# Attention and gated FFN in one kernel: two x tiles turned by DMA instead of on TensorE, six FFN units in halves, one load and four stores moved

## The chip, the cores and the metric

The kernel runs on one core of one Trainium2 chip. The metric is the device time of one execution in microseconds (us); lower is better. One execution in each case was also recorded by the profiler. The record marks each run as fast or slow by its time and its granted clock. Engines: PE is TensorE, PEld its weight loads, DVE is VectorE, ACT is ScalarE, POOL is GpSimd, SP is SyncE, whose work in these traces is to issue DMAs.

## The reference

```python
# q, k, v: (8 batches, 8 heads, 576, 64) float32
phi(x) = concat(relu(x) * cos, relu(x) * sin)        # by position in the sequence
kv  = phi(k)^T v ;  z = sum over s of phi(k)
x   = (phi(q) kv) / (phi(q) z + 1e-6)                # -> (4608 tokens, 512)
out = (gelu(x w_gate) * (x w_val)) w_out             # w_gate, w_val: 512 x 1536; w_out: 1536 x 512
```

A batch has 576 tokens. The FFN works on nine blocks of 512 tokens, so a block straddles two batches. Block 1 is the last 64 tokens of batch 0 and the first 448 of batch 1.

## The kernel before

Per batch: `prep` makes phi(q) and phi(k) (cosine half on VectorE, sine half on ScalarE); q is transposed to `qT`; `kv_unit` makes kv; `nm_unit(b, t)` makes one tile x(b, t) of 128 tokens; the tile must be transposed ("turned") to become columns of `xT`, the moving operand of the FFN. Per block: 12 units `gv_unit` (gate and value matmuls, gelu on ScalarE, product on VectorE), then four output tiles `o_part`.

There are two ways to turn a tile. One holds TensorE (0.22 us a tile in the trace before) and needs a copy out of PSUM by ScalarE (L361, 0.37 to 0.63 us each there); the other is a DMA in SP's queue:

```python
def turn_x(b, t):
    x = xs.pop((b, t))
    for blk, c, o, m in pieces(b, t):                  # a tile that straddles blocks: two pieces
        nc.sync.dma_start_transpose(out=xT_block(blk)[:, :, c:c + m], in_=x[o:o + m, :])

def turn_x_pe(b, t, to, copy):
    x = xs.pop((b, t))
    p = bank16(to)[:, 0:CT * 128].rearrange("p (c n) -> p c n", c=CT)
    for ct in range(CT):                               # four transposes
        nc.tensor.transpose(out=p[:, ct, :], in_=x[:, ct * 128:(ct + 1) * 128], identity=ident)
    for blk, c, o, m in pieces(b, t):
        copy(xT_block(blk)[:, :, c:c + m], p[:, :, o:o + m])
```

A unit can run in halves, `gv_unit(n, unit, half * HALF, HALF)`: first the left 256 columns of several units, then the right 256. In block 1 the left half needs tiles 0 and 1 of batch 1, the right half tiles 1, 2 and 3 (of tile 3 the first 64 tokens; the rest belongs to block 2).

The stretch between the blocks, and the start of block 1 (before):

```python
    # GpSimd's queue: weights, q(1), k(1), v(1), then the loads of batch 2
    for name in ("q", "k"):
        for m in (0, 2):
            load(nc.gpsimd, name, 2, m, m + 2)
    for m in (0, 2):
        load(nc.gpsimd, "v", 2, m, m + 2)
    # ... block 0 ...
    order = (
        [("q", 0, 2, 0, 6), ("q", 2, 4, 0, 7), ("o", 0, 0), ("k",), ("o", 1, 0)]
        + [("q", 0, 2, 4, 2), ("o", 2, 0), ("q", 2, 4, 4, 3), ("o", 3, 0), ("o", 0, 4)]
        + [("q8", 2), ("o", 1, 4), ("o", 2, 4), ("kv",), ("q2", 0, 2), ("o", 3, 4)]
        + [("nm", 0, 2), ("o", 0, 8), ("nm", 1, 6), ("o", 1, 8), ("xt", 0, 4), ("nm", 2, 2)]
        + [("q2", 2, 3), ("o", 2, 8), ("xt", 1, 5), ("nm", 3, 6), ("q2", 3, 4), ("o", 3, 8)]
        + [("xt", 2, 4)]
    )
    # "q": transposes of phi(q(1)); "o": a third of an output tile; "q2": preparation of q(2);
    # "nm": nm_unit(1, t); "xt": turn_x_pe(1, t, bank)
    for m in (0, 2):
        load(nc.sync, "q", 3, m, m + 2)
    # ... block 1, unit jt:
            heads = (0, 2, 4, 2)[n] if n < 4 else 0          # units in halves
                    if n == 1:
                        j = JA + 2 * jt + i                  # preparation of q(2), one position
                        prep("q", b, 1, (j,), eng=nc.scalar)
                        prep("q", b, 0, (j,))
                        if jt == i == 0:
                            turn_x_pe(1, 3, 5, act_copy)     # tile 3 after the first half unit
                if n == 1 and jt == 2:
                    # (last position of q(2)) ...
                    turn_q(b)                                # q(2)'s turn, two DMA transposes by SP
                    nm_unit(1, NT - 1)
```

Each `o_part` that ends a tile also issues the stores of the tile before (`flush`), in SP's queue.

## Time and profile before

| | before |
|---|---|
| median of 3 runs, known at the prediction | 326.14 us (325.64 to 326.65) |
| median of 6 runs, with the result | 326.61 us (325.64 to 327.38) |
| span of the profiled run | 323.9 us |
| TensorE busy | 316.8 us, 98% |
| chain of waits on TensorE | 93% |

The first lines are from the page of the kernel before: busy time with share of the span and number of instructions; then the chain of work that ended last, by engine (a q behind an engine's name is its instruction queue, "issue" is time in which nothing that the profile shows was waited for); then the group of the gate matmuls (count, busy us, mean ns, idle time before them).

```profile
PE 316.8 (98%) x2451; PEld 164.5 (51%) x2451; DVE 170.3 (53%) x407; ACT 159.3 (49%) x336; POOL 26.0 (8%) x43
PE 93%; DMA 2%; DVE 2%; SPq 1%; issue 0%; DVEq 0%
L400 PE MATMUL ps<-xT,wg_sb 128*128 128x512 bf16 (+1 forms) x456 | 110.2, 364 | 0.0
```

With 98% of the span busy and 93% of the chain, TensorE bounds the kernel. Only what comes off TensorE's own sequence, or makes it stand still, moves the time.

The timeline of TensorE before, where block 1 starts (start, duration with the modelled tail, instruction):

```profile
53.44 1.02 PE L430 MATMUL ps<-wo_sb,hT 128*128 128x512 bf16 x4
54.30 0.39 PE L357 MATMUL ps<-ident,x_sb 128*128 128x128 bf16 x4
54.53 0.60 PE L400 MATMUL ps<-xT,wg_sb 128*128 128x256 bf16 x4
54.96 0.60 PE L400 MATMUL ps<-xT,wv_sb 128*128 128x256 bf16 x4
55.40 0.39 PE L357 MATMUL ps<-ident,x_sb 128*128 128x128 bf16 x4
55.62 0.60 PE L400 MATMUL ps<-xT,wg_sb 128*128 128x256 bf16 x4
56.06 0.60 PE L400 MATMUL ps<-xT,wv_sb 128*128 128x256 bf16 x4
56.62 0.60 PE L400 MATMUL ps<-xT,wg_sb 128*128 128x256 bf16 x4
```

Read such a list by its start times: the groups overlap (those of half matmuls last 0.60 us in the list and start 0.44 us apart), so a group costs the distance to the next start. Turning tile 2 costs the distance from 54.30 to 54.53, 0.22 us before rounding, and tile 3 the same. A group of four half matmuls costs 0.44 us, so a half unit 0.87. The third half unit starts 0.12 us late.

### The profile page before, as it was taken

To read this page: it belongs to the slowest core of one execution; us is meant where nothing else is said; L and a number is where in the kernel's file an instruction comes from. 1 tells how busy PE (TensorE), PEld (TensorE's weight loads), DVE (VectorE), ACT (ScalarE), POOL (GpSimd) and SP (SyncE) were. 2 spreads that over 40 slices of the span, in tenths; PEclk is the share of its full clock that TensorE was granted. 3 is DMA by queue.
4 is the path that set the end of the run, shared out by engine and by line. 5 is a ranking of instruction groups with operands and counts; after the bars stand their busy time and mean duration, and the time that the engine had idled before them with its cause. 6 is when DMAs were issued, how large, how long until landed. Compare 5 with 4: busy or idle time off the path is not lost.

```text
span 323.9 us, 6340 instructions
## 1 busy us (share of the span) xinstructions
PE 316.8 (98%) x2451; PEld 164.5 (51%) x2451; DVE 170.3 (53%) x407; ACT 159.3 (49%) x336; POOL 26.0 (8%) x43
## 2 busy tenths in 40 slices
PE   8899999999999999999999999999999999999995
PEld 3574556555754564545544554445544444444443
DVE  5854677759665952793586348544532222222211
ACT  7864858946466832673457336633222332222220
POOL 6684410000000000000000000000000000000000
PEclk9999999999999999999999999999999999999999
DMA  7999999842999689938957990543431111111124
GB/s 274 249 186 273 297 352 366 230 111 51 323 216 354 166 147 383 201 83 251 330 96 157 383 232 1 137 102 78 85 73 33 34 32 32 35 32 32 34 65 98
DMA packets 69102, 53.57 MB, mean 165 GB/s; under 512 B 45392, under 2 KB 54352, under 8 KB 69072
## 3 DMA queue, kind: packets, MB, share of 16 engines
q1 hardware_dynamic: 59264, 41.23, 48.1%
q0 software_dynamic: 9648, 11.80, 15.7%
q8 instruction: 19, 0.31, 0.4%
q10 hardware_dynamic: 160, 0.13, 0.1%
q14 instruction: 11, 0.09, 0.1%
HBM read 37.75 MB, written 9.44 MB: 146 GB/s over the span
## 4 chain that ended last, share of the span: by engine, by line
PE 93%; DMA 2%; DVE 2%; SPq 1%; issue 0%; DVEq 0%
PE ps L400 57%; PE ps L430 28%; PE ps L282 3%; PE ps L241 3%; DMA vf<-in_v_dram 2%; PE ps L204 1%; PE ps L372 1%; PE ps L697 1%; SPq L80 1%; PE ps L357 0%; DVE qp L162 0%; DVE x_sb L322 0%; DVE vx L179 0%; DVE x_sb L295 0%; DVE qT L486 0%
## 5 line engine op out<-in xcount | busy, mean ns | idle before, releaser
L409 DVE TENSOR_TENSOR hT<-gel,ps 128x512 bf16<-128x512 f32 (+1 forms) x114 | 74.1, 650 | 128.9 <-PE ps L400 126.0
L408 ACT ACTIVATE gel<-ps 128x512 f32<-128x512 f32 (+1 forms) x114 | 64.8, 569 | 109.7 <-PE ps L400 108.0
L400 PE MATMUL ps<-xT,wv_sb 128*128 128x512 bf16 (+1 forms) x456 | 110.2, 364 | 0.0
L400 PE MATMUL ps<-xT,wg_sb 128*128 128x512 bf16 (+1 forms) x456 | 110.2, 364 | 0.0
L430 PE MATMUL ps<-wo_sb,hT 128*128 128x512 bf16 x420 | 105.8, 379 | 0.0
L400 PEld LDWEIGHTS <-wv_sb 128*128 128x128 bf16 x456 | 44.6, 98 | 47.0
L400 PEld LDWEIGHTS <-wg_sb 128*128 128x128 bf16 x456 | 44.0, 98 | 46.1
L430 PEld LDWEIGHTS <-hT 128*128 128x128 bf16 x420 | 38.3, 98 | 39.4
L439 ACT COPY o_sb<-ps 128x512 f32<-128x512 f32 x34 | 19.9, 587 | 29.9 <-PE ps L430 27.6
L160 ACT ACTIVATE qp<-qf,sin_t 128x256 bf16<-128x256 f32 x72 | 32.0, 501 | 0.4 <-DMA qf<-in_q_dram 0.4
L160 ACT ACTIVATE kp<-kf,sin_t 128x256 bf16<-128x256 f32 (+1 forms) x73 | 29.9, 479 | 0.9 <-DMA kf<-in_k_dram 0.9
L295 DVE TENSOR_TENSOR x_sb<-ps,rec 128x512 bf16<-128x512 f32 x38 | 26.3, 691 | 1.3
L162 DVE TENSOR_SCALAR qp<-qf,cos_t 128x256 bf16<-128x256 f32 x71 | 21.8, 353 | 2.3 <-DMA qf<-in_q_dram 2.3
L282 PEld LDWEIGHTS <-qT 128*128 128x128 bf16 x304 | 14.6, 98 | 7.9 <-ACT qT L486 0.3
L162 DVE TENSOR_SCALAR kp<-kf,cos_t 128x256 bf16<-128x256 f32 x63 | 18.3, 349 | 0.0
L282 PE MATMUL ps<-kv_sb,qT 128*128 128x65 bf16 x304 | 16.0, 194 | 0.0
L179 DVE CAST vx<-vf 128x1152 bf16<-128x1152 f32 (+1 forms) x15 | 12.0, 804 | 0.8 <-DMA vf<-in_v_dram 0.8
L250 ACT CAST kv_sb<-ps 128x260 bf16<-128x260 f32 x14 | 4.6, 383 | 12.9 <-PE ps L241 12.9
L241 PEld LDWEIGHTS <-kp 64*128 64x128 bf16 x504 | 8.5, 95 | 3.0 <-issue 3.0
L140 PE MATMUL ps<-dummy 128*128 128x512 bf16 x27 | 8.4, 457 | 1.5 <-POOL dummy L113 1.5
L241 PE MATMUL ps<-vx,kp 64*128 64x65 bf16 x504 | 9.3, 191 | 0.0
L294 DVE RECIPROCAL rec<-den 128x8 f32<-128x8 f32 x38 | 7.7, 203 | 1.3
(60 smaller groups left out, 100.6 us busy)
## 6 DMA issues: line engine op xcount, KB each, us to landing
out_dram<-o_sb SPq DMA_DIRECT2D x70, 128.0 KB, 2.6
kf<-in_k_dram SPq DMA_DIRECT2D x12, 576.0 KB, 6.2
vf<-in_v_dram SPq DMA_DIRECT2D x12, 576.0 KB, 8.3
qf<-in_q_dram SPq DMA_DIRECT2D x10, 576.0 KB, 5.0
qf<-in_q_dram POOLq DMA_DIRECT2D x4, 576.0 KB, 12.2
kf<-in_k_dram POOLq DMA_DIRECT2D x4, 576.0 KB, 12.5
vf<-in_v_dram POOLq DMA_DIRECT2D x4, 576.0 KB, 12.8
wg_sb<-in_moe_w_gate_dram POOLq DMA_DIRECT2D x6, 256.0 KB, 6.4
```

The costliest lines, as they stand in the source:

```text
L140: nc.tensor.matmul(bank(to), lhsT=dummy[:, 0:128], rhs=dummy, start=True, stop=True)
L160: nc.scalar.activation(o, i, AF.Relu, scale=tab[:, j:j + 1])
L162: (eng or nc.vector).tensor_scalar(o, i, 0.0, tab[:, j:j + 1], op0=ALU.max, op1=ALU.mult)
L179: copy(vx_tiles[b % 2][:, m0:m1, j0:j1, 0:D], staged["v", b][:, m0:m1, j0 * D:j1 * D].rearrange("p m (j d) -> p m j d", d=D),)
L241: nc.tensor.matmul(bank(6 + i)[:, m * (D + 1):(m + 1) * (D + 1)], lhsT=kp[rr, m, j, :], rhs=vx[rr, m, j, :], start=(j == 0), stop=(j == R ...
L282: nc.tensor.matmul(bank(b0 + h // 4)[:, (h % 4) * (D + 1):(h % 4 + 1) * (D + 1)], lhsT=q_cols(b, t, h), rhs=kv_sb[b][:, h // 2, h % 2, :], ...
L295: nc.vector.tensor_tensor(x, nm[:, :, :, 0:D], rec[:, :, :, None].to_broadcast([128, 2, 4, D]), op=ALU.mult,)
L400: nc.tensor.matmul(bank(b0 + g)[:, 0:w], lhsT=wt[:, ct, js], rhs=xt[:, ct, c0:c0 + w], start=(ct == 0), stop=(ct == CT - 1),)
L408: nc.scalar.activation(gel[:, 0:w], bank(b0)[:, 0:w], AF.Gelu)
L409: nc.vector.tensor_mul(hT[n][:, jt, c0:c0 + w], gel[:, 0:w], bank(b0 + 1)[:, 0:w])
L430: nc.tensor.matmul(bank(to), lhsT=hT[n][:, jt, tt * 128:(tt + 1) * 128], rhs=wo_sb[:, jt, :], start=(jt == 0), stop=(jt == JT - 1),)
L439: copy(o_sb, bank(to))
```

## The change

The intent is to take two groups of transposes off TensorE (x tiles 2 and 3 of batch 1) and give them to the DMA. A DMA turn takes longer (2.3 to 2.5 us from issue to landing in the trace before, for those issued from 69 to 80 us), so the units that need these tiles must start later (six units in halves, left halves first), and SP's queue must be free when the turns are issued (behind bulk loads in it a turn took 10.0 us there, issued at 96.4 us): q(3)'s load goes to the GpSimd queue, of block 0's stores tile 0's go ahead of the turns, tile 1's behind them, and those of tiles 2 and 3 behind q(2)'s turn. The preparation of q(2) is rearranged so that q(2)'s turn is issued after unit 1 instead of unit 2, and k(2) is prepared position by position. The core of the diff (cut where marked):

```diff
+    def flush(n=4):                                   # stores in parts
+        for i, o_sb in stores[:n]:
             store((nc.sync, nc.sync), i, o_sb)
+        del stores[:n]
@@ o_part
-            flush()
+            if i == 1 or n > 0:
+                flush()
@@ GpSimd queue
+    for name, b in (("q", 2), ("k", 2), ("v", 2), ("q", 3)):
         for m in (0, 2):
+            load(nc.gpsimd, name, b, m, m + 2)
@@ order
-        + [("q8", 2), ("o", 1, 4), ("o", 2, 4), ("kv",), ("q2", 0, 2), ("o", 3, 4)]
-        + [("nm", 0, 2), ("o", 0, 8), ("nm", 1, 6), ("o", 1, 8), ("xt", 0, 4), ("nm", 2, 2)]
-        + [("q2", 2, 3), ("o", 2, 8), ("xt", 1, 5), ("nm", 3, 6), ("q2", 3, 4), ("o", 3, 8)]
-        + [("xt", 2, 4)]
+        + [("q8", 2), ("o", 1, 4), ("o", 2, 4), ("kv",), ("o", 3, 4)]
+        + [("nm", 0, 2), ("o", 0, 8), ("nm", 1, 6), ("q2", 0, 2), ("o", 1, 8), ("xt", 0, 4), ("nm", 2, 2), ("xd", 2)]
+        + [("o", 2, 8), ("xt", 1, 5), ("q2", 2, 3), ("nm", 3, 6), ("xd", 3), ("q2", 3, 4), ("o", 3, 8)]
+        if what == "xd":
+            turn_x(1, a[0])
+    flush(1)
-    for m in (0, 2):
-        load(nc.sync, "q", 3, m, m + 2)
@@ block 1
-            heads = (0, 2, 4, 2)[n] if n < 4 else 0
+            heads = (0, 6, 4, 2)[n] if n < 4 else 0
-                        if jt == i == 0:
-                            turn_x_pe(1, 3, 5, act_copy)
+                if n == 1 and jt == 1:
+                    turn_q(b)
                 if n == 1 and jt == 3:
                     turn_x(1, NT - 1)
+                    flush()
... (preparation of q(2) in units 0 and 1, of k(2) from unit 2 on)
```

More of the change, by code (lines that the diff above doesn't have):

```diff
@@ L420, in store @@
             eng.dma_start(out=dst, in_=o_sb[64 * n:64 * n + 64, c0:c1])
-    def flush():
-        for i, o_sb in stores:
+    def flush(n=4):
+        for i, o_sb in stores[:n]:
             store((nc.sync, nc.sync), i, o_sb)
-        stores.clear()
+        del stores[:n]
     def o_part(i, jts, to, copy):
@@ L474 @@
     load_wo(8, 4)
-    for name in ("q", "k"):
+    for name, b in (("q", 2), ("k", 2), ("v", 2), ("q", 3)):
         for m in (0, 2):
-            load(nc.gpsimd, name, 2, m, m + 2)
-    for m in (0, 2):
-        load(nc.gpsimd, "v", 2, m, m + 2)
+            load(nc.gpsimd, name, b, m, m + 2)
     def turn_j(b, m0, m1, js, to, copy):
@@ L581 @@
             turn_x_pe(1, a[0], a[1], act_copy)
-    for m in (0, 2):
-        load(nc.sync, "q", 3, m, m + 2)
+        if what == "xd":
+            turn_x(1, a[0])
+    flush(1)
     def prep_third(name, b, i):
@@ L623 @@
                     gv_unit(n, unit, half * HALF, HALF)
-                    if n == 1:
-                        j = JA + 2 * jt + i
-                        prep("q", b, 1, (j,), eng=nc.scalar)
-                        prep("q", b, 0, (j,))
-                        if jt == i == 0:
-                            turn_x_pe(1, 3, 5, act_copy)
-            if jt % 3 == 1:
+                    if n == 1 and jt < 2:
+                        js = ((4,), (5,), (6,), (7, 8))[2 * jt + i]
+                        prep("q", b, 1, js, eng=nc.scalar)
+                        prep("q", b, 0, js)
+                    if n == 1 and jt > 1:
+                        j = 2 * jt - 4 + i
+                        prep("k", b, 0, (j,))
+                        prep("k", b, 1, (j,), eng=nc.scalar)
+            if jt % 3 == 1 and n > 1:
                 flush()
             if b < B:
+                if n == 1 and jt == 1:
+                    turn_q(b)
                 if n == 1 and jt == 2:
-                    prep("q", b, 0, (R - 1,))
-                    prep("q", b, 1, (R - 1,), eng=nc.scalar)
-                    turn_q(b)
                     nm_unit(1, NT - 1)
@@ L653 @@
                     kv_unit(b)
-                i = jt - 1 - n if n <= 2 else -1
-                if 0 <= i < 3:
-                    prep_third("k", b, i)
+                if n == 1 and jt == 6:
+                    prep("k", b, 0, (R - 1,))
+                    prep("k", b, 1, (R - 1,), eng=nc.scalar)
+                if n == 2 and 3 <= jt < 6:
+                    prep_third("k", b, jt - 3)
                 i = 2 * (jt - 5) if n == 1 else jt - (4 if n == 2 else 0)
```

## The prediction

> **What bounds the kernel.** TensorE: busy 316.8 of 323.9 us (98%, busy times), 93% of the chain of waits; the granted clock is full in every slice. In the timeline of 39 to 62 us, the stretch that the change touches, each of its groups starts where the one before ends; I find two gaps of some 0.1 us (before batch 1's kv unit at 47.23 and the third half unit at 56.62). ScalarE is slack on average (49%) but full from 52 to 58 us (table by windows).
>
> **What the change does, costed from the timeline.**
> 1. Tiles 2 and 3 are no longer turned on TensorE: each group of four transposes holds it 0.22 us (54.30 to 54.53, 55.40 to 55.62). Removed: 0.45 us, on the critical path. ScalarE loses three copies out of PSUM, off the path.
> 2. Four more units run in halves. A half unit takes 0.87 us, a whole one 1.73: 0.02 us more each, 0.05 to 0.1 us in all, on the path. This buys time: the second column half, which alone needs tiles 2 and 3, starts six half units (5.2 us) into the block, about 59.5 us instead of 56.5.
> 3. Three DMA transposes are added in SP's queue (tile 3 in two pieces), 1.2 us of issue each. On an idle queue such a turn lands 2.3 to 2.5 us after issue (69 to 80 us); behind bulk loads in SP's own queue it took 10.0 (at 96.4). So moving q(3)'s load away, and holding back stores, matters. The GpSimd queue ran dry about 54.3 us; q(3)'s 1.18 MB at the 425 GB/s of 50 to 52 us add 2.8 us: it runs to about 57, beside the turns. [...] the turns should be slowed, not queued behind; this trace has only stores as a parallel: 4.5 us under load against 2.6.
> 4. q(2)'s turn is issued about 60 us instead of 61.5, and k(2)'s preparation is spread. Both have slack: q(2)^T is first read about 72 us, kv(2) runs at 69.
>
> **Deadline.** x of tile 2 should be ready about 53.4 us, of tile 3 about 54.7. With 4 to 5 us under load they land by 58 to 59.5, against a need at 59.5: little slack; one chance in three of a stall of 0.3 to 1 us. Second tight place: the first half unit needs ScalarE's copy of tile 1 just as TensorE arrives (54.1 against 54.3).
>
> **Sum.** -0.45 + 0.08, and +0.1 for expected stalls: -0.3 us. From 326.14 I predict 325.8 us, range 325.1 to 326.9. Faster by over 2%: 1%; within 2%: 98%; slower by over 2%: 1%. The affected stretch is 20 us of a full TensorE; 6.5 us cannot come of it.
>
> **What would show it.** 2,475 matmuls instead of 2,451 (8 transposes fewer, 32 half matmuls more); 37 turns of x by DMA instead of 34; 118 gelus instead of 114. The first half unit starts about 54.3 us instead of 54.53; block 2's first unit about 77.7 instead of 78.04, and everything later keeps that offset; span about 323.6. The three turns land 3 to 5 us after issue. If TensorE idles before the seventh half unit, released by the DMA of xT, the deadline failed; if it idles before the first or third on ScalarE, the sines did it.
>
> **What would make it wrong.** Turns much slower beside the GpSimd queue's loads (8 to 10 us) would stall TensorE 3 to 4 us: 329. q(3)'s load delaying v(2) or k(2) would show as VectorE waiting before their preparation. A start-up that differs by chance would hide all of it: the three runs of before spread by 1.0 us.

## More of the kernel before

The DMA queues before, in the window from 53 to 54 us (queue, packets, MB, share of the 16 engines' time). q0 is the GpSimd queue, q1 SP's:

```profile
q0 software_dynamic: 79, 0.30, 75.4%
q1 hardware_dynamic: 44, 0.08, 21.7%
```

From 50 to 53 us q1 had no packet at all, although SP had issued two stores at 51.3 and 51.9 us. They landed at 55.98 and 56.28.

## The result, and the profile after

| | before | after |
|---|---|---|
| median of 6 runs | 326.61 us (325.64 to 327.38) | 326.56 us (326.15 to 326.95) |
| ratio | | 1.0000, 95% interval 0.9982 to 1.0018 |
| span of the profiled run | 323.9 us | 324.0 us |

A ratio here and below is the mean time of one kernel's fast runs over the mean of the other's of the same rounds, so it is not quite the ratio of the medians. All outputs are right.

The time is the same within 0.18%, which is 0.6 us; the predicted 0.3 us is less than this measurement can tell. So the traces have to say what happened. The same lines of the page after, and from its list of groups the line of the gate matmuls (busy, mean ns, idle before and what ended it):

```profile
PE 314.1 (97%) x2438; PEld 167.4 (52%) x2475; DVE 171.2 (53%) x411; ACT 159.0 (49%) x337; POOL 29.5 (9%) x45
PE 90%; DMA 6%; issue 1%; ACT 1%; POOL 1%; DVE 0%; SPq 0%; DVEq 0%
L400 PE MATMUL ps<-xT,wg_sb 128*128 128x512 bf16 (+1 forms) x463 | 109.9, 357 | 1.6 <-DMA xT<-x_sb 0.9
```

The weight loads count 2,475 matmuls, as predicted (37 matmul records are missing from the trace). The chain of waits now has 6% on DMA (v(0)'s load, a weight load and the turn of x, 2% each), and in the list of groups an idle time of 0.9 us ended by the DMA of xT appears, where the same line before had 0.0. The timeline of TensorE after shows where:

```profile
53.28 0.81 PE L430 MATMUL ps<-wo_sb,hT 128*128 128x512 bf16 x3
53.93 0.60 PE L400 MATMUL ps<-xT,wg_sb 128*128 128x256 bf16 x4
54.37 0.60 PE L400 MATMUL ps<-xT,wv_sb 128*128 128x256 bf16 x4
...
58.73 0.60 PE L400 MATMUL ps<-xT,wv_sb 128*128 128x256 bf16 x4
59.17 0.42 PE L282 MATMUL ps<-kv_sb,qT 128*128 128x65 bf16 x8
60.46 0.60 PE L400 MATMUL ps<-xT,wg_sb 128*128 128x256 bf16 x4 [0.87 <-DMA xT<-x_sb]
```

The two groups of transposes (L357) are gone and the first six half units follow each other without a gap. Then the seventh, which is the first to need tiles 2 and 3, starts at 60.46 us. The x unit before it (L282) costs 0.26 us, so it could have started at 59.43: TensorE lost 1.03 us.

What SP issued after:

```profile
50.93 1.47 SPq L420 DMA_DIRECT2D out_dram<-o_sb  x2
53.37 3.88 SPq L349 DMA_TRANSPOSE xT<-x_sb  x3
57.34 1.18 SPq L420 DMA_DIRECT2D out_dram<-o_sb  x2
59.67 8.09 SPq L193 DMA_TRANSPOSE qT<-qp  x2
```

The three turns, issued at 53.37, 54.76 and 56.01, landed at 60.11, 60.33 and 60.54 us. From the view of the line that issues them, window 53 to 61:

```profile
DMA to landing us min/median/max: 4.5/5.6/6.7
```

Three DMAs issued 1.3 us apart that land 0.2 us apart did not take 6.7, 5.6 and 4.5 us each. This looks like a wait for one common event; the experiments test which.

To compare traces, take two numbers from TensorE's timeline. The start of the first of q(1)'s 16 transposes, which comes before anything that the change touches, is **S**; what lies before it is called the start-up here (two profiles of the changed kernel have S at 38.71 and 40.24). The time from there to block 2's first half unit is the **stretch**; it holds everything that the change does. What follows block 2's start took 245.7 to 246.0 us in all traces but one (246.3).

| | S | stretch | S + stretch |
|---|---|---|---|
| before | 39.08 | 38.96 | 78.04 |
| after | 38.71 | 39.49 | 78.20 |

So in its profiled run the changed kernel was 0.53 us slower in the stretch that it was meant to shorten, and an early start hid most of it. The sum is: -0.45 for the transposes, +0.08 for more halves, -0.12 for the gap before the third half unit that is gone, +1.03 for the wait: +0.54.

### The profile page after: what moved, and what is told of

Same layout as the page of the kernel before. It is cut to its first block, busy times and chain, and to the rows that moved or that the text cites. A ratio compares the mean times of both kernels' runs of the same rounds, so it can differ in the third digit from the quotient of the medians.

```text
span 324.0 us, 6372 instructions
## 1 busy us (share of the span) xinstructions
PE 314.1 (97%) x2438; PEld 167.4 (52%) x2475; DVE 171.2 (53%) x411; ACT 159.0 (49%) x337; POOL 29.5 (9%) x45
## 3 DMA queue, kind: packets, MB, share of 16 engines
q1 hardware_dynamic: 59840, 40.32, 48.0%
## 4 chain that ended last, share of the span: by engine, by line
PE 90%; DMA 6%; issue 1%; ACT 1%; POOL 1%; DVE 0%; SPq 0%; DVEq 0%
PE ps L400 55%; PE ps L430 27%; PE ps L282 3%; PE ps L241 3%; DMA vf<-in_v_dram 2%; DMA wv_sb<-in_moe_w_val_dram 2%; DMA xT<-x_sb 2%; PE ps L700 1%; PE ps L372 1%; PE ps L204 1%; SPq L80 0%; POOL wg_sb L94 0%; PE ps L357 0%; ACT qp L160 0%; POOL gate L459 0%
## 5 line engine op out<-in xcount | busy, mean ns | idle before, releaser
L430 PE MATMUL ps<-wo_sb,hT 128*128 128x512 bf16 x401 | 103.0, 379 | 1.4 <-issue 0.8
L400 PEld LDWEIGHTS <-wv_sb 128*128 128x128 bf16 x472 | 46.2, 98 | 45.4
L400 PEld LDWEIGHTS <-wg_sb 128*128 128x128 bf16 x472 | 45.6, 98 | 45.8 <-DMA xT<-x_sb 1.0
L282 PEld LDWEIGHTS <-qT 128*128 128x128 bf16 x304 | 14.6, 98 | 7.7 <-ACT qT L485 0.3
L282 PE MATMUL ps<-kv_sb,qT 128*128 128x65 bf16 x304 | 16.0, 194 | 0.1
```

What stands on the lines that cost most here:

```text
L282: nc.tensor.matmul(bank(b0 + h // 4)[:, (h % 4) * (D + 1):(h % 4 + 1) * (D + 1)], lhsT=q_cols(b, t, h), rhs=kv_sb[b][:, h // 2, h % 2, :], ...
L400: nc.tensor.matmul(bank(b0 + g)[:, 0:w], lhsT=wt[:, ct, js], rhs=xt[:, ct, c0:c0 + w], start=(ct == 0), stop=(ct == CT - 1),)
L430: nc.tensor.matmul(bank(to), lhsT=hT[n][:, jt, tt * 128:(tt + 1) * 128], rhs=wo_sb[:, jt, :], start=(jt == 0), stop=(jt == JT - 1),)
```

## The experiments

Theory A: the turns are late because of the bulk loads in the GpSimd queue, which q(3) prolongs; without the lateness the change is worth about 0.5 us. Rival B: the turns are late for another reason (SP's issue, tile 0's stores ahead of them, v(2)'s load alone). Rival C: the loss lies in other parts of the change. In the expectations "the measure" to the x unit of block 2 is the stretch plus 1.74 us (before: 40.70).

All traces, with the point of time at which the last packet of the GpSimd queue ended and the first turn of x landed:

| kernel | S | stretch | wait of TensorE in it | GpSimd queue's last packet | first turn landed | median us | ratio to before, 95% |
|---|---|---|---|---|---|---|---|
| before | 39.08 | 38.96 | none | 55.21 | | 326.61 | |
| r_before | 39.16 | 38.97 | none | 55.87 | | 326.77 | 1.0000 (0.9978 to 1.0022) |
| changed kernel | 38.71 | 39.49 | 1.03, turns | 59.07 | 60.11 | 326.56 | 1.0000 (0.9982 to 1.0018) |
| r_after | 40.24 | 38.47 | none | 59.52 | 60.57 | 326.59 | 1.0004 (0.9981 to 1.0027) |
| e1_q3_sp | 39.34 | 38.47 | none | 55.83 | 57.44 | 326.21 | 0.9994 (0.9965 to 1.0022) |
| r_e1 | 40.45 | 39.83 | 1.2, q(2)'s turn | 55.71 | 57.63 | 327.25 | 1.0020 (0.9994 to 1.0046) |
| e2_half8 | 39.60 | 39.04 | 0.3, VectorE | 59.65 | 60.71 | 326.26 | 0.9992 (0.9968 to 1.0016) |
| e3_turns_pe | 39.10 | 39.22 | none listed | 59.65 | | 326.54 | 1.0004 (0.9981 to 1.0027) |
| e4_double | 39.37 | 42.85 | 2.85, turns | 61.74 | 62.60 | 329.91 | 1.0097 (1.0068 to 1.0126) |
| e5_act_queue | 38.99 | 39.03 | 0.57, turns | 58.93 | 59.83 | 326.24 | 0.9987 (0.9966 to 1.0007) |
| e6_half8_cast | 40.32 | 38.51 | none | 59.20 | 60.13 | 326.55 | 0.9991 (0.9977 to 1.0005) |
| e7_act_later | 40.77 | 40.45 | 1.8, q(2)'s turn | 56.64 | 58.28 | 327.70 | 1.0026 (1.0003 to 1.0048) |
| e8_no_store | 39.48 | 38.47 | none | 58.72 | 59.63 | 326.19 | 0.9984 (0.9968 to 1.0001) |
| e9_best | 40.00 | 38.69 | none listed | 59.10 | 60.20 | 326.36 | 0.9992 (0.9975 to 1.0009) |

(Waits for turns of x are distances between starts, less the work in between; the others are as the list of waits has them, which does not list gaps under 0.15 us. Its entries of 0.2 us for "issue" are left out: they stand where a matmul record is missing.)

### r_after: the changed kernel again

No edit.

> The changed kernel again, unaltered. In its first profile TensorE stood still for about 1.0 us before the seventh half unit of block 1 (59.43 to 60.46 us), released by the DMA of xT; the three turns landed 6.7, 5.6 and 4.5 us after issue. If that is its nature and not chance, a second profile shows the same gap within 0.3 us, and the stretch of TensorE from the group of 16 transposes of q(1) (38.71 there) to block 2's first half unit (78.20) lasts 39.5 us again, against 39.0 before. Ratio to before between 0.999 and 1.002.

Measured: no gap. The expectation failed, and this failure taught the most. TensorE's timeline, r_after:

```profile
60.26 0.60 PE L400 MATMUL ps<-xT,wv_sb 128*128 128x256 bf16 x4
60.70 0.42 PE L282 MATMUL ps<-kv_sb,qT 128*128 128x65 bf16 x8
60.96 0.60 PE L400 MATMUL ps<-xT,wg_sb 128*128 128x256 bf16 x4
```

Here the start-up was 1.5 us later (S 40.24 instead of 38.71), so TensorE came to the seventh half unit at 60.96 us instead of 59.43. The turns landed at 60.57 and 60.76, hardly later than in the first profile (60.11, 60.33). They follow the clock of the loads (GpSimd's last packet at 59.52 instead of 59.07), TensorE follows its start-up, and the wait is the difference. Without the wait the stretch is 38.47 us: 0.49 less than before, which is the predicted -0.45 + 0.08 and the closed gap of 0.12.

### e1_q3_sp: q(3)'s load back in SP's queue, behind the turns

```diff
-    for name, b in (("q", 2), ("k", 2), ("v", 2), ("q", 3)):
+    for name, b in (("q", 2), ("k", 2), ("v", 2)):
@@
     flush(1)
+    for m in (0, 2):
+        load(nc.sync, "q", 3, m, m + 2)
```

> Only q(3)'s load goes back to SP's queue, but behind the three turns and tile 1's stores. Theory A (the turns are starved by the GpSimd queue's bulk loads, which q(3) prolongs from 54.3 to about 57.5 us): the turns land by about 57.5 to 59 us, 3 to 5 us after issue, the 1.0 us gap before the seventh half unit is gone or under 0.2 us, the stretch is 38.5 us, and the time falls by 0.8 to 1.0 us against the changed kernel. Rival B (the turns are late by themselves, by SP's issue of 1.2 us each, by the store of tile 0 ahead of them, or by v(2)'s load alone): they still land at about 60 us and at least 0.6 us of the gap stays. Rival C (q(2)'s turn now stands behind q(3)) would show as a new wait of TensorE after 70 us.

Measured: the GpSimd queue ran dry at 55.83 us instead of 59.07, and the turns landed within 2.3 to 3.4 us of their issue. The line of their issue, e1_q3_sp, window 53 to 58:

```profile
DMA to landing us min/median/max: 2.3/2.4/3.4
```

No gap, stretch 38.47. This is theory A: v(2)'s load, SP's issue and tile 0's stores were all still there. In the times, -0.1% with an interval that holds 1.0; the expected gain of 0.8 us and more was worked out for an early start-up and is not seen.

### r_e1: the same again

No edit against e1_q3_sp.

> The same kernel as e1_q3_sp, a second time, as the candidate for the best version. Turns land 2.3 to 3.5 us after issue, no gap before the seventh half unit whether the start-up is early or late, the time from the group of 16 transposes of q(1) to the nm unit in block 2's first pair of halves is 40.2 us (40.21 in the first profile; before 40.70, changed kernel 41.24 and 40.21). Ratio to before 0.998 to 0.9995, its interval probably still holding 1.0.

Measured: the turns again landed early, but the time was 0.2% above before and TensorE waited further on. Timeline of TensorE, r_e1:

```profile
72.96 0.19 PE L282 MATMUL ps<-kv_sb,qT 128*128 128x65 bf16 x1
74.34 0.40 PE L282 MATMUL ps<-kv_sb,qT 128*128 128x65 bf16 x7 [1.19 <-DMA qT<-qp]
```

and of SP:

```profile
60.35 1.07 SPq L80 DMA_DIRECT2D qf<-in_q_dram  x2
61.60 9.62 SPq L193 DMA_TRANSPOSE qT<-qp  x2
```

q(2)'s turn stands behind q(3)'s 1.18 MB in the same queue; its second half landed at 74.30 us, while the first x unit of batch 2 wanted it at 73.0. In e1_q3_sp it landed at 71.24 and was in time for 71.85. So the part of the change that moves q(3) to the GpSimd queue has a purpose: it protects q(2)'s turn. Rival C, named in the expectation of e1_q3_sp, is true of this variant. The expectation of a ratio below 1 failed.

### e2_half8: eight units in halves

```diff
-            heads = (0, 6, 4, 2)[n] if n < 4 else 0
+            heads = (0, 8, 4, 2)[n] if n < 4 else 0
@@
-                    if n == 1 and jt > 1:
+                    if n == 1 and 1 < jt < 6:
```

> Eight units in halves instead of six, the rest as in the changed kernel: the turns are needed 1.75 us later (61.2 instead of 59.4 us), for 0.04 us more of matmuls. Whatever makes the turns late (theory A or rival B), they land at 60.1 to 60.5 us as before, the gap is gone, the stretch is 38.5 us and the time falls by 0.8 to 1.0 us against the changed kernel. If the gap does not close, TensorE was not waiting for the turns.

Measured: the turns landed at 60.71 to 61.13, a little later than expected, and TensorE did not wait for them. The mean time was 0.1% below before, with an interval that holds 1.0; the expected 0.8 us is not seen. Another wait came instead, 0.3 us at 68.28 us for VectorE, which the 1.4 us cast of v(2) held; 0.12 us more was lost ahead of the change, at q(1)'s last transposes. The stretch of 39.04 does not confirm the expected 38.5.

### e3_turns_pe: the turns on TensorE, the rest as changed

The two lines of `order` are cut to their ends.

```diff
-  ("nm", 2, 2), ("xd", 2)]
+  ("nm", 2, 2)]
-  ("nm", 3, 6), ("xd", 3), ("q2", 3, 4), ("o", 3, 8)]
+  ("nm", 3, 6), ("q2", 3, 4), ("o", 3, 8), ("xt", 2, 4)]
@@ in block 1, after each half unit
+                    if n == 1 and jt == i == 0:
+                        turn_x_pe(1, 3, 5, act_copy)
```

> Tiles 2 and 3 turned on TensorE again as before the change, at the same two places, everything else as in the changed kernel. Theory A and B alike: no gap at the seventh half unit, 0.45 us of transposes more: the stretch is 38.9 to 39.1 us, the time 0.4 to 0.6 us below the changed kernel and level with before (ratio 0.999 to 1.001). If the gap stays, or the time is above the changed kernel's, the loss lies in another part of the change (halves, order of q(2)'s and k(2)'s preparation).

Measured: stretch 39.22, ratio 1.0004. There is no wait for turns. Against the 38.47 of the changed kernel without its wait, the two groups on TensorE cost 0.75 us: 0.45 for themselves, 0.08 at the ninth half unit, 0.17 before the fourth, and 0.05 elsewhere. The copies that belong to them fall into ScalarE's full stretch; that these copies cause the small gaps is likely but not shown. The 0.05 us lies mostly at q(1)'s transposes, ahead of the change. The other parts of the change alone bring nothing. The changed kernel's time was expected 0.4 to 0.6 us above this one and is level with it.

### e4_double: twice the suspected cost

```diff
-    for name, b in (("q", 2), ("k", 2), ("v", 2), ("q", 3)):
+    for name, b in (("q", 2), ("k", 2), ("v", 2), ("q", 3), ("k", 3)):
@@
-                    loads(3, ("k", "v"))
+                    loads(3, ("v",))
```

> The suspected cost doubled: k(3)'s 1.18 MB follow q(3) in the GpSimd queue (instead of SP's queue at the end of block 1), the rest as in the changed kernel. Theory A, in the form that the traces so far suggest (SP's queue moves nothing on an engine as long as the GpSimd queue has packets for it): at about 420 GB/s that queue runs dry 2.8 us later, at about 60 us, tile 0's stores and the three turns land together at about 62.5 to 64 us whenever they were issued, and TensorE stands still for 2 to 3.5 us before the seventh half unit; ratio to before 1.005 to 1.010, which is more than the noise of start-up. If the queues took turns by packets, the turns would land at 60 to 61 us as with q(3) alone, the gap staying under 1.2 us.

Measured: +0.97%, clear of the noise, and as theory A expected it. The GpSimd queue's last packet came 2.7 us later (61.74), the turns landed at 62.60, 62.81 and 63.02, and TensorE waited 2.85 us. The time from issue to landing, e4_double, window 53 to 61:

```profile
DMA to landing us min/median/max: 6.4/7.4/8.6
```

But the stretch grew by 4.38 us over 38.47, not by 2.85. TensorE's timeline, e4_double, has the other 1.53:

```profile
62.94 1.01 PE L400 MATMUL ps<-xT,wg_sb 128*128 128x256 bf16 x4 [2.69 <-DMA xT<-x_sb]
63.75 1.06 PE L400 MATMUL ps<-xT,wv_sb 128*128 128x256 bf16 x4
64.60 1.06 PE L400 MATMUL ps<-xT,wg_sb 128*128 128x256 bf16 x4
65.45 0.93 PE L400 MATMUL ps<-xT,wv_sb 128*128 128x256 bf16 x4
66.22 0.60 PE L400 MATMUL ps<-xT,wg_sb 128*128 128x256 bf16 x4
```

After the wait the first four groups took 3.28 us instead of 1.75. The table by windows of the same run shows the granted clock just after the busy times of the engines (the number before the DMA share and the GB/s): 0.68 from 62 to 64 us and 0.50 from 64 to 66 us. Worked out from these and the 0.97 of the next window, with the clock taken as 1.00 or 0.50 throughout, it was halved from about 62.7 to 66.1 us, so by this estimate it fell before the wait was over.

```profile
62.00:64.00 2.00, 1.06 (x6) 0.78 (x7) 0.00 (x0) 0.01 (x1) 0.00 (x0) 0.68 1.21 291
64.00:66.00 2.00, 2.00 (x11) 1.45 (x10) 0.69 (x2) 1.07 (x4) 0.00 (x0) 0.50 0.76 176
```

By the same estimate the clock fell about 2.6 us after TensorE's work before the wait ended (60.09 us). The waits of 1.2 us in r_e1 and 1.8 us in e7_act_later left the granted clock at 1.00 (windows from 72 to 76 us). At what length of a wait the clock falls was not tested. The wait of 2.85 us was paid more than once: it cost 4.38 us.

How the queues shared the engines in this run, window 58 to 59 us:

```profile
q0 software_dynamic: 97, 0.39, 95.2%
q1 hardware_dynamic: 95, 0.02, 10.6%
```

As many packets of SP's queue as of GpSimd's, but about a sixteenth of the bytes (24 KB against 392 KB). In the trace's packet records GpSimd's loads go in packets of 4,608 bytes (median 178 ns each on its engine) and the turns in packets of 256 bytes, 1,024 of them for the two tiles. So in this window the two queues shared the engines by packets, 97 to 95. An estimate from these numbers: 64 turn packets on each of 16 engines, if spread evenly and each after one load packet of 178 ns, are over 11 us. By this estimate the turns could not finish beside a full backlog of loads. In the traces with q(3) in the GpSimd queue the first turn landed 0.9 to 1.1 us after that queue's last packet.

How the turns were held to the very end is inferred, because the packet records do not name the engine. In the changed kernel's own trace the GpSimd queue and SP's queue moved 72 and 72 packets from 55 to 56 us (SP's were the store's), but 31 and 334 from 57 to 58 and 9 and 173 from 58 to 59. The window from 57 to 58 us, changed kernel:

```profile
q1 hardware_dynamic: 334, 0.08, 102.4%
q0 software_dynamic: 31, 0.11, 26.0%
```

So most turn packets moved with no load packet in between, and yet the first turn did not land before 60.11: it seems to have waited for its share on the few engines that still had loads. The turns did not hold up the loads in their turn: in e3_turns_pe, without any turn of x, the GpSimd queue's last packet came as late (59.65).

### e5_act_queue: q(3) through ScalarE's hardware queue

```diff
-    for name, b in (("q", 2), ("k", 2), ("v", 2), ("q", 3)):
+    for name, b in (("q", 2), ("k", 2), ("v", 2)):
@@ in "q8"
                 cast_v(1, m, m + 2, dve_copy)
+                load(nc.scalar, "q", 3, m, m + 2)
```

> q(3)'s load is issued by ScalarE in its own hardware queue at about 45.5 us, while it waits for kv(1), instead of by GpSimd; the rest as in the changed kernel. If a backlog in the GpSimd queue holds up every hardware queue, q(3) moves nothing until v(2) has drained at about 54 us, lands at 57 to 58 us, and shares the engines with the turns, which then land at 57 to 59.5 us, earlier than the 60.1 to 60.5 us of the changed kernel: a gap of at most 0.3 us, stretch 38.5 to 38.8 us in the measure used above. If hardware queues and the GpSimd queue take turns by packets, q(3) lands at 51 to 53 us and v(2) some 2 us later than before.

Measured: neither half of the expectation quite. ScalarE issued at 43.6 us and its queue (q10) moved its first packet at 47.25; from then on it and the GpSimd queue moved about as many packets each (61 to 67 in every us from 48 to 55). Window 50 to 51 us, e5_act_queue:

```profile
q0 software_dynamic: 65, 0.25, 61.8%
q10 hardware_dynamic: 66, 0.15, 38.4%
```

So the GpSimd backlog did not shut out q10 (66 packets to 65 in this us), and the stronger form of theory A is refuted. But v(2), sharing with q(3), ended at 58.93 instead of about 55.5, the turns landed at 59.83 to 60.53, hardly earlier than in the changed kernel, and a wait of 0.57 us stayed. So giving the same bytes to another queue did not free the turns; taking them out of that time (e1_q3_sp) did.

A point that stays open: in all seven traces with q(3) loaded early and a store first in SP's queue (this run, e4_double, both profiles of the changed kernel, e2_half8, e3_turns_pe, e6_half8_cast) the first packet of that queue moved 3.8 us after the store's issue. In the two traces where a turn came first (e8_no_store, e9_best) it was 2.3 and 1.4 us, and in the five without q(3) ahead 1.2 to 2.5 us. What sets this delay was not tested.

### r_before: the kernel before again

No edit.

> The kernel before, unaltered, for the noise and for a second profile: ratio to itself within 0.999 to 1.001, the time from the group of 16 transposes of q(1) to the nm unit in block 2 again 40.7 us within 0.15, while the point of time of that group, which start-up sets, may lie anywhere from 38.5 to 40.5 us.

Measured: stretch 38.97 against 38.96, S 39.16. The stretch can be trusted to a few hundredths where nothing waits; the times cannot be, to less than 0.2%.

### e6_half8_cast: eight units in halves, v(2)'s cast in two pieces

```diff
 (heads and preparation of k(2) as in e2_half8)
-                if n == 1 and i == 0:
-                    cast_v(b, 0, 4, dve_copy)
+                if n == 1 and i in (0, 2):
+                    cast_v(b, i, i + 2, dve_copy)
```

> Eight units in halves, as in e2_half8, and the cast of v(2), which held VectorE for 1.4 us in one piece there, in two pieces after units 5 and 6. In e2_half8 the gap for the turns was gone but TensorE waited 0.26 us on VectorE (68.28 us) behind that cast; that wait should go. From the group of 16 transposes of q(1) to the nm unit in block 2: 40.3 us (before 40.70, e2_half8 40.78 with also 0.12 us lost at the fourth group of q(1)'s transposes, which may come by chance), whatever the start-up. Ratio to before 0.998 to 0.9995: a gain of 0.4 us is inside the noise of start-up.

Measured: stretch 38.51, no wait; the wait for VectorE is gone. Ratio 0.9991, not clear of 1. The start-up was late here (S 40.32), so this profile alone would not have shown a wait for turns anyway; that the deadline has moved by 1.75 us follows from the start times.

### e7_act_later: q(3) by ScalarE after unit 2

```diff
-    for name, b in (("q", 2), ("k", 2), ("v", 2), ("q", 3)):
+    for name, b in (("q", 2), ("k", 2), ("v", 2)):
@@
                 if n == 1 and jt == 2:
                     nm_unit(1, NT - 1)
+                    for m in (0, 2):
+                        load(nc.scalar, "q", 3, m, m + 2)
```

> q(3)'s load is taken out of the GpSimd queue and issued by ScalarE after unit 2 of block 1 (about 60 us), when the turns of x are through, and in a queue in which q(2)'s turn does not stand behind it. Theory A says: the turns land 2.3 to 3.5 us after issue as in e1_q3_sp, no gap at the seventh half unit; and q(2)'s turn, which in the repeat of e1_q3_sp stood behind q(3) in SP's queue and cost TensorE 1.19 us at 74.3, lands by 71 us: no wait. The measure is 40.2 us. If sharing the engines with q(3) slows q(2)'s turn past 72.3 us, a wait of TensorE for qT remains.

Measured: the turns of x landed 2.3 to 2.9 us after issue, and the last sentence of the expectation came true: beside q(3), q(2)'s turn landed at 75.24 us and TensorE waited 1.8 us for it at 73.5. Ratio 1.0026; besides e4_double it is the only variant whose interval excludes 1 (1.0003 to 1.0048), by so little that chance alone could do it; the wait in the trace is the stronger evidence. With r_e1 this shows the trade: q(3)'s load collides with the turns of x when it is early (a wait of 1.03 us in the first profile of the changed kernel) and with q(2)'s turn when it is late (1.2 us in r_e1, 1.8 us here).

### e8_no_store: tile 0's store behind the turns

```diff
-            if i == 1 or n > 0:
+            if n > 0:
```

> The changed kernel without the store of tile 0 ahead of the turns in SP's queue (it goes behind them). Rival B: the two stores, whose first packet moved 3.8 us after issue and which landed at 56.8 and 59.4 us, hold up the turns behind them; then the turns land well before the GpSimd queue's last packet, at 57 to 59 us, and the gap goes. Theory A: the turns need all engines clear of the GpSimd queue, whose last packet ended at 58.9 to 59.7 us in all traces with q(3) in it; the first turn lands 0.8 to 1.2 us after that packet, at 59.8 to 60.7 us, and with an early start-up (the group of 16 transposes before 39.5 us) a gap of 0.2 to 1 us stays.

Measured: the first turn landed at 59.63, 0.9 us after the GpSimd queue's last packet (58.72), as theory A has it. With no store ahead, the turns were not earlier in relation to that packet than in the changed kernel; so the store ahead was not what held them behind the loads, and that part of rival B falls. The loads themselves ended at 58.72 and 59.10 us in the two traces without the store ahead (this one and e9_best), and at 59.07 to 59.65 in the five with it; whether the store's 256 KB cost that difference was not tested. There was no gap: TensorE came at 60.20 us, the second turn was there at 59.93. Theory A had foreseen a gap of 0.2 us or more with an S under 39.5; S was 39.48, so by the letter that part of the expectation failed, if on the edge.

### e9_best: both edits together

The edits of e6_half8_cast and e8_no_store.

> Both edits that left no gap, together: eight units in halves with v(2)'s cast in two pieces (e6_half8_cast) and tile 0's store behind the turns (e8_no_store). The turns are then due 1.75 us later than in the changed kernel and land 0.8 to 1.2 us after the GpSimd queue's last packet, so there is no wait of TensorE for them whatever the start-up; the measure is 40.25 us against 40.70 before, and the ratio to before lies between 0.9975 and 0.9995, with an interval that may still hold 1.0 because start-up alone moves a run by 1 us.

Measured: no wait for turns; ratio 0.9992, interval 0.9975 to 1.0009; stretch 38.69, of which 0.2 us was lost at q(1)'s last transposes, ahead of all that was edited (0.12 us in e2_half8). Why that group sometimes starts late was not followed up. By the traces this version is 0.3 to 0.5 us shorter than before; by the times it is not shown to be faster.

## Why the prediction was right or wrong

The prediction held: 326.56 us lies within 325.1 to 326.9, and "within 2%" was right. This says little. The range also holds both medians of the kernel before (326.14 and 326.61), so no effect at all would have passed too; and the middle of it, 325.8, came out 0.76 us too low. The overlap of the turns with the loads was wrong, and whether it cost TensorE anything in an execution was left to the start-up. Point by point:

1. **The gain.** "Removed: 0.45 us" and "0.05 to 0.1 us" added: right. With the wait absent (r_after, e1_q3_sp, e8_no_store) the stretch is 38.47 us against 38.96 and 38.97 before: -0.49 us, with the closed gap of 0.12.
2. **The deadline.** "A need at 59.5", right (59.43). "One chance in three of a stall of 0.3 to 1 us": it was named, with the right place and the right releaser. In the two profiles of the changed kernel it was 1.03 and 0 us.
3. **The step that failed** is "the turns should be slowed, not queued behind ... with 4 to 5 us under load they land by 58 to 59.5". They took 6.7, 5.6 and 4.5 us and landed at 60.11 to 60.54 (second profile: 5.7, 4.4 and 3.5 us, 60.57 to 61.02). The step was the author's estimate. In the later traces the queues did share the engines by packets (65 to 66 in e5_act_queue, 97 to 95 in e4_double, each in 1 us), but that did not make the turns merely slower: the two tiles' turns are 1,024 packets of 256 bytes, and by the estimate under e4_double, with each behind a load packet of 4,608 bytes, they would take over 11 us beside a full backlog. And the parallel was misread. The stores before took 4.7, 4.4, 3.5 and 3.2 us, falling as they were issued later, and all landed after the GpSimd queue had nearly run dry; that reads as no rate under load but as a wait for the end of the loads (no packet of SP's queue moved from 50 to 53 us). The end itself was mis-sized too: "it runs to about 57" was 59.07 us; the queue did not stop at once, its packets thinned out (31 and 9 in the last two microseconds before 59).
4. **"Behind bulk loads in SP's own queue it took 10.0 ... so moving q(3)'s load away ... matters"**: it matters, though not for these turns, which stood ahead of q(3) in e1_q3_sp and landed 2.3 to 3.4 us after issue. What it protects is q(2)'s turn (landed at 74.30 us in r_e1, 75.24 in e7_act_later), which the prediction had called slack. In the changed kernel it was slack: landed at 69.33 us, first read at 72.25.
5. **The checks.** 2,475 matmuls, 37 turns, 118 gelus, the first half unit 0.23 us earlier in relation to S: right. "Block 2's first unit about 77.7": 78.20 and 78.70. "Span about 323.6": 324.0 and 324.5.
6. **The sum.** -0.3 us cannot be confirmed or refuted by the times. An estimate from the traces: over the 14 profiles S was 39.6 us in the mean, so TensorE would need the turns at 60.3, and in three traces with the DMA traffic of the changed kernel (that kernel twice, and e2_half8) the second turn landed at 60.3 to 60.9. That is a wait of 0.1 to 0.7 us in a mean start-up, against a gain of 0.49. By this estimate the gain went there, wholly or in good part; the times cannot show it.
7. **"A start-up that differs by chance would hide all of it"**: right, and more than expected. S ranged from 38.71 to 40.77 us. The base of three runs (326.14) was 0.5 us under the median of six.

What stays open: what makes S vary by 2 us; the delay of 3.8 us before a queue's first packet; how the last loads hold the turns, engine by engine; the 0.1 to 0.2 us at q(1)'s last transposes; and whether any of these versions is faster in the times by the 0.1% that their traces show.

## What to carry to other kernels

When several DMAs are issued one after another and land together, do not read their latencies as a rate: look for the event that released them all, here the end of the bulk loads in another queue (GpSimd's last packet at 59.07 us, the three turns from 60.11 to 60.54). A transfer of small packets beside one of large packets got its share by packets here (e4_double, 1 us: 95 packets with 0.02 MB beside 97 with 0.39 MB), and with q(3) in the GpSimd queue the first DMA transpose landed 0.9 to 1.1 us after the last load packet. So count a DMA transpose beside such loads as done when they are done: its landing followed the loads, its deadline the compute engine. Before believing an effect of a few tenths of a microsecond, measure from a point behind the start-up (S ranged over 2 us here) to a point behind the change, in more than one trace; if the wait depends on which side was early, one trace shows only one case.
